# Loads of q, k and v split from one transfer for two head pairs into one per pair: a study of a linear-attention and token-mixing kernel

## Chip, cores, metric

One core of one Trainium2 chip. The metric is device time of one execution in microseconds (us). The kernel before takes 133.86 us (median of 3 runs, 133.42 to 133.96). "Span" is the profiled execution, a little shorter than the timed one.

## The reference

```python
# q, k, v: (8, 8, 576, 64) f32: batch, heads, sequence, head size
r = np.maximum(x, 0); phi(x) = concat([r * cos_w, r * sin_w])   # cos, sin of pi/2 * position / 576
kv  = einsum('bhsf,bhsd->bhfd', phi(k), v);  z = sum(phi(k), axis=2)
num = einsum('bhsf,bhfd->bhsd', phi(q), kv)
x   = num / (einsum('bhsf,bhf->bhs', phi(q), z)[..., None] + 1e-6)   # then heads side by side: (8, 576, 512)
wq, wk = x @ w_q, x @ w_k                                            # 512 -> 64
mixed  = einsum('bst,btd->bsd', einsum('bsd,btd->bst', wq, wk) / 8, x)
out    = np.maximum(mixed, 0) @ w_out                                # (8, 576, 512) f32
```

29.6 MB are read and 9.4 MB written.

## The kernel before

The work is cut into 16 units H; one unit is four heads, two "pairs" of two heads. A raw tile of one tensor and one unit has 128 partitions, 2 pairs, 576 columns of f32: 128 x 2 x 2304 B = 576 KB, with the two pairs side by side in a partition. It comes in one DMA. Six raw buffers are used in turn. All but a few DMAs are issued by SyncE, loads and stores in one queue.

```python
inp     = ctx.enter_context(tc.tile_pool(name="inp", bufs=PLAN["nraw"]))        # 6 raw buffers
outpool = ctx.enter_context(tc.tile_pool(name="outpool", bufs=PLAN["nout"]))    # 10 result buffers
...
def load(H, parts=((0, C9),), names=("q", "k", "v"), engs=()):
    ...
    b, h0 = divmod(2 * H, NPAIR)
    for nm in names:
        raw[nm, H] = inp.tile([P, 2, HC], FP32, name="raw")
    for lo, hi in parts:
        for nm in names:
            eng = nc.scalar if lo == 0 and nm in engs else nc.sync
            eng.dma_start(raw[nm, H][:, :, lo * D:hi * D],
                          srcs[nm][b][:, h0:h0 + 2, lo * D:hi * D])
...
def raw_c(nm, H, lo, hi):                 # what a cast reads: columns of BOTH pairs
    return raw[nm, H].rearrange("p i (c d) -> p c i d", c=C9)[:, lo:hi]
...
def store(bp, rt, qs):                    # a result tile of 128 x 512 f32: two DMAs of 64 partitions
    for hi in range(2):
        qs[hi].dma_start(
            dataclasses.replace(out, offset=out.offset + out_dest(bp, rt, hi),
                                ap=[[C9 * DM, 64], [1, DM]]),
            o_sbs[bp, rt][64 * hi:64 * hi + 64, :])
```

POOL (GpSimd) casts each raw tile, DVE multiplies k by the cosines, PE does the rest. The order of all instructions is fixed by a planner in the kernel.

Of the kernel before, what the change touches and what calls it, by code (L numbers as in the profile page):

```python
# [5 lines left out]

# [174 lines left out]
def kernel(  # L181
# [12 lines left out]
    B, NH, S, D = q.shape  # L194
# [37 lines left out]
    srcs = {}  # L232
# [3 lines left out]
    raw = {}  # L236
    CS = ((0, 5), (5, C9))

    def load(H, parts=((0, C9),), names=("q", "k", "v"), engs=()):
        if H >= NB:  # L240
            return
# [3 lines that stand above are left out]
        for lo, hi in parts:  # L245
            for nm in names:
                eng = nc.scalar if lo == 0 and nm in engs else nc.sync
                eng.dma_start(raw[nm, H][:, :, lo * D:hi * D],
                              srcs[nm][b][:, h0:h0 + 2, lo * D:hi * D])

    load(0, parts=CS, engs=("k",))

    warm = consts.tile([P, 512], BF16)
# [302 lines left out]
    def emit(n, eng, m):  # L556
        kind, b, j = n[0], n[1], n[2] if len(n) > 2 else 0
        if kind == "load":
            load(j, names=(b,))
        elif kind == "load_w":  # L560
            load_w(b)
# [91 lines left out]
```

## Time and profile before

| | before |
|---|---|
| time, median | 133.86 us |
| span of the profiled run | 130.8 us |
| mean PE clock granted | 0.974 of full |
| transfers in all; issued by SyncE from 40 to 90 us | 126; 61 |
| last load of k lands | 94.7 us |

The prediction below shows the views that it rests on; where it speaks of the first or second "pair" or of one "pair" of loads, it means a unit H. Beside those views, the page of the kernel before has these lines: PE's busy time, the PE clock in 40 slices (tenths of full speed), and the groups of issues (KB of one transfer, median us from issue to landing).

```profile
PE 105.8 (81%) x2279; PEld 61.8 (47%) x2279; DVE 93.8 (72%) x153; ACT 78.5 (60%) x154; POOL 76.8 (59%) x121
PEclk9999999999959999999999999999999999999995
raw<-in_k_dram SPq DMA_DIRECT2D x15, 576.0 KB, 7.3
out_dram<-o_sb SPq DMA_DIRECT2D x67, 128.0 KB, 5.3
```

The view by windows (window, its length, busy us of PE, PEld, DVE, ACT and POOL with counts, then the granted PE clock, the DMA share and GB/s):

```profile
48.00:56.00 8.00, 7.78 (x162) 4.56 (x156) 7.65 (x13) 5.07 (x12) 7.83 (x10) 1.00 1.05 400
64.00:72.00 8.00, 7.69 (x194) 4.89 (x193) 7.57 (x14) 4.83 (x11) 6.22 (x8) 1.00 1.03 394
40.00:90.00 50.00, 45.41 (x1123) 28.12 (x1122) 43.96 (x72) 35.12 (x73) 41.10 (x52) 1.00 1.03 375
```

### The profile page before, as it was taken

Reading aid. Unit: us, or ns where it says so; the run is one execution under the profiler, and the core shown is the slowest. Engines: PE = TensorE matmul, PEld = TensorE weight load, DVE = VectorE, ACT = ScalarE, POOL = GpSimd, SP = SyncE. Lnnn points to the kernel's source line nnn. Section 1 sums busy time; section 2 is a strip of 40 time slices with the busy share of each in tenths; the row PEclk is TensorE's granted clock in tenths of the full one; section 3 lists DMA queues with packets and bytes.
Section 4 is the critical chain, followed back from the end, with each engine's and each line's share of the span. In section 5 each row is a group of like instructions: output and inputs, shape, how many; then the busy total and the mean of one; then the engine's idle time right before and its main releaser. Section 6 shows DMA issues by size and latency. Waiting matters only on the chain.

```text
span 130.8 us, 5363 instructions
## 1 busy us (share of the span) xinstructions
PE 105.8 (81%) x2279; PEld 61.8 (47%) x2279; DVE 93.8 (72%) x153; ACT 78.5 (60%) x154; POOL 76.8 (59%) x121
## 2 busy tenths in 40 slices
PE   5947685885699989986999699889947999899930
PEld 2325253563546546643756366556624664443300
DVE  1065979689994999959999987989659876346200
ACT  6950063658756796639557595787637865655440
POOL 7728988896779999975697876885371000000000
PEclk9999999999959999999999999999999999999995
DMA  3999999999999999999999999999974034837973
GB/s 88 369 383 394 345 310 403 394 388 390 389 393 388 374 391 396 401 378 376 316 393 413 368 359 378 383 373 295 382 214 87 5 80 89 177 75 167 211 226 110
DMA packets 21239, 39.40 MB, mean 301 GB/s; under 512 B 3040, under 2 KB 4576, under 8 KB 21216
## 3 DMA queue, kind: packets, MB, share of 16 engines
q1 hardware_dynamic: 20544, 38.08, 85.0%
q10 hardware_dynamic: 672, 0.98, 2.5%
q8 instruction: 18, 0.29, 0.9%
q14 instruction: 5, 0.04, 0.1%
HBM read 29.62 MB, written 9.44 MB: 299 GB/s over the span
## 4 chain that ended last, share of the span: by engine, by line
PE 43%; DMA 23%; DVE 14%; ACT 5%; POOL 5%; issue 4%; SPq 2%; ACTq 1%; POOLq 0%
PE ps L532 19%; DMA raw<-in_k_dram 12%; DMA raw<-in_q_dram 9%; PE ps L422 5%; PE ps L462 5%; PE ps L397 5%; DVE kp L361 4%; DVE qpt_buf L389 4%; PE ps L492 3%; POOL rk L348 3%; PE ps L447 2%; PE ps L383 2%; DVE x_sb L435 2%; PE ps L508 2%; POOL rq_buf L348 2%
## 5 line engine op out<-in xcount | busy, mean ns | idle before, releaser
L532 PE MATMUL ps<-wo_sb,mix_sb 128*128 128x512 bf16 x144 | 37.3, 386 | 2.0 <-issue 1.7
L348 POOL TENSOR_SCALAR rq_buf<-raw 128x640 bf16<-128x640 f32 (+1 forms) x32 | 26.2, 835 | 9.3 <-DMA raw<-in_q_dram 7.9
L373 POOL TENSOR_SCALAR v_buf<-raw 128x640 bf16<-128x640 f32 (+1 forms) x30 | 27.1, 920 | 7.4 <-DMA raw<-in_v_dram 6.6
L361 DVE TENSOR_TENSOR kp<-rk,cossin 128x2304 bf16<-128x2304 bf16 (+2 forms) x17 | 22.5, 1324 | 11.3 <-ACT rk L346 6.1
L335 ACT COPY o_sb<-ps 128x512 f32<-128x512 f32 x32 | 18.8, 586 | 15.8 <-PE ps L532 12.9
L435 DVE TENSOR_TENSOR x_sb<-ps,rec 128x640 bf16<-128x640 f32 x32 | 26.4, 824 | 1.1
L389 DVE TENSOR_TENSOR qpt_buf<-ps,cst 128x1152 bf16<-128x1152 bf16 x32 | 22.6, 747 | 0.0
L348 POOL TENSOR_SCALAR rk<-raw 128x640 bf16<-128x640 f32 (+1 forms) x30 | 19.5, 669 | 4.2 <-DMA raw<-in_k_dram 2.7
L422 PEld LDWEIGHTS <-qpt_buf 64*128 64x128 bf16 x640 | 14.3, 95 | 14.0 <-issue 13.2
L422 PE MATMUL ps<-kv_sb,qpt_buf 64*128 64x65 bf16 x320 | 16.3, 193 | 4.2 <-DVE x_sb L435 3.7
L532 PEld LDWEIGHTS <-mix_sb 128*128 128x128 bf16 x144 | 11.9, 98 | 15.6 <-issue 4.1
L335 ACT COPY xT_buf<-ps 128x640 bf16<-128x640 bf16 (+1 forms) x25 | 15.7, 650 | 3.0 <-PE ps L447 1.7
L422 PE MATMUL ps<-kv_sh,qpt_buf 64*128 64x65 bf16 x320 | 16.3, 192 | 1.1 <-issue 0.2
L397 PE MATMUL ps<-v_buf,kp 64*128 64x65 bf16 x576 | 13.1, 190 | 3.8 <-DVE qpt_buf L389 2.9
L520 ACT ACTIVATE mix_sb<-ps 128x576 bf16<-128x576 f32 x24 | 14.7, 657 | 2.4 <-PE ps L508 2.4
L397 PEld LDWEIGHTS <-kp 64*128 64x128 bf16 x576 | 10.6, 94 | 8.2 <-issue 3.4
L335 ACT CAST kv_sb<-ps 128x260 bf16<-128x260 f32 x13 | 4.9, 378 | 12.4 <-PE ps L397 12.2
L508 PE MATMUL ps<-wT_buf,kx 64*128 64x288 bf16 x32 | 8.5, 292 | 2.6 <-ACT mix_sb L520 1.9
L258 PE MATMUL ps<-warm 128*128 128x512 bf16 x31 | 9.4, 441 | 1.5 <-DVE warm L254 1.5
L383 PE MATMUL ps<-ident,rq_buf 64*128 64x64 bf16 x288 | 8.1, 192 | 2.6 <-POOL rq_buf L348 1.3
L433 DVE RECIPROCAL rec<-ps 128x10 f32<-128x10 f32 x32 | 6.8, 213 | 4.0 <-PE ps L426 3.8
L462 PE MATMUL ps<-xT_buf,wqk_sb 128*128 128x288 bf16 x64 | 9.2, 287 | 0.0
(51 smaller groups left out, 115.8 us busy)
## 6 DMA issues: line engine op xcount, KB each, us to landing
raw<-in_q_dram SPq DMA_DIRECT2D x15, 576.0 KB, 7.1
raw<-in_k_dram SPq DMA_DIRECT2D x15, 576.0 KB, 7.3
raw<-in_v_dram SPq DMA_DIRECT2D x15, 576.0 KB, 7.2
out_dram<-o_sb SPq DMA_DIRECT2D x67, 128.0 KB, 5.3
wo_f<-in_moe_w_out_dram SPq DMA_DIRECT2D x1, 1024.0 KB, 10.2
out_dram<-o_sb ACTq DMA_DIRECT2D x5, 128.0 KB, 2.9
raw<-in_k_dram ACTq DMA_DIRECT2D x1, 320.0 KB, 4.5
raw<-in_q_dram SPq DMA_DIRECT2D x1, 320.0 KB, 4.2
```

Of the source, the lines that this page charges most:

```text
L335: nc.scalar.copy(dst, src)
L348: eng.tensor_scalar(dst, src, FMAX, 0.0, op0=ALU.min, op1=ALU.max)
L361: nc.vector.tensor_mul(kp[H][:, 2 * lo:2 * hi], rks[H][:, lo:hi].rearrange("p c i d -> p (c i) d").unsqueeze(2) .to_broadcast([P, 2 * (hi ...
L373: eng.tensor_scalar(dst, src, 1.0, 1.0, op0=ALU.mult, op1=ALU.mult)
L389: nc.vector.tensor_mul(qpt_bufs[H % 2][:, r, :, D:SLOTS * D], bank_h(K0 + r)[:, 0:1, 0:HC].to_broadcast([P, 2, HC]), cst)
L397: nc.tensor.matmul(bank(K0 + r)[:, 0, i * (D + 1):(i + 1) * (D + 1)], kp[H][half_rows(r), 2 * c + i, :, :], v_bufs[H % 3][half_rows(r), c, ...
L422: nc.tensor.matmul(nb[t][:, u, :], qpt_bufs[H % 2][rows, r, w, u * P:(u + 1) * P], mv, start=(u == 0 and w == 0), stop=False)
L435: nc.vector.tensor_tensor(xv[:, h, r], nv[:, :, :, 0:D], rec.to_broadcast([P, 2, SC, D]), op=ALU.mult)
L462: nc.tensor.matmul(bank(m + nh)[:, 0, 0:hs], wqk_sb[:, dmc, :, :], xT_bufs[b % 2][:, dmc, nh * hs:(nh + 1) * hs], start=(dmc == 0), stop=( ...
L508: nc.tensor.matmul(bank(m + r)[:, 0, 0:hs], kxs[b][half_rows(r), i * P:(i + 1) * P], rhs, start=True, stop=True)
L520: nc.scalar.activation(dst, src, AF.Relu, scale=scale_moe)
L532: nc.tensor.matmul(bank(m)[:, 0, :], mixs[bp][:, dmc, rt * P:(rt + 1) * P], wo_sb[:, dmc, :], start=(dmc == 0), stop=(dmc == NDM - 1))
```

## The change

Each 576 KB load becomes two of 288 KB, one per pair. The idea is a finer grain: shorter transfers that land sooner.

```diff
-                eng.dma_start(raw[nm, H][:, :, lo * D:hi * D],
-                              srcs[nm][b][:, h0:h0 + 2, lo * D:hi * D])
+                for i in range(2) if H else (slice(0, 2),):
+                    eng.dma_start(raw[nm, H][:, i, lo * D:hi * D],
+                                  srcs[nm][b][:, h0:h0 + 2, lo * D:hi * D][:, i])
```

The first unit keeps its loads. (The diff also adds an unused `import random`.)

More of the change, by code (lines that the diff above doesn't have):

```diff
@@ L4 @@
 import os
+import random
 from contextlib import ExitStack
```

## The prediction

> **What bounds the kernel now.** I read the page first. Its DMA row and its rate row cut the span in two.
>
> ```profile
> DMA  3999999999999999999999999999974034837973
> GB/s 88 369 383 394 345 310 403 394 388 390 389 393 388 374 391 396 401 378 376 316 393 413 368 359 378 383 373 295 382 214 87 5 80 89 177 75 167 211 226 110
> DMA packets 21239, 39.40 MB, mean 301 GB/s; under 512 B 3040, under 2 KB 4576, under 8 KB 21216
> ```
>
> A slice is 130.8/40 = 3.27 us. From about 3 to 95 us the 16 DMA engines are at least 90% busy and move some 380 GB/s; then the loads are over and a tail of PE work remains (PE is busy 7.92 of the 8 us from 104 to 112 in the view by windows). Next I asked whether anyone waits for these loads. POOL casts every raw tile from the second pair on; its timeline towards the end of the loads (start, duration, instruction; in brackets the idle time before it and what ended that):
>
> ```profile
> 88.66 1.80 POOL L373 TENSOR_SCALAR v_buf<-raw 128x640 bf16<-128x640 f32 x2 [0.76 <-DMA raw<-in_v_dram]
> 93.39 1.30 POOL L348 TENSOR_SCALAR rq_buf<-raw 128x640 bf16<-128x640 f32 x2 [2.94 <-DMA raw<-in_q_dram]
> 94.86 1.29 POOL L348 TENSOR_SCALAR rk<-raw 128x640 bf16<-128x640 f32 x2 [0.17 <-DMA raw<-in_k_dram]
> 96.93 1.78 POOL L373 TENSOR_SCALAR v_buf<-raw 128x640 bf16<-128x640 f32 x2 [0.78 <-DMA raw<-in_v_dram]
> ```
>
> POOL starts each cast when its load lands. The chain that ended last has the same piece in it (start, duration, what):
>
> ```profile
> 86.64 0.25 SPq L248
> ...
> 86.99 7.73 DMA raw<-in_k_dram
> ...
> 94.86 1.30 POOL rk L348 x2
> ...
> 96.19 1.36 DVE kp L361
> ```
>
> So the end is set by when the last loads land, about 93 to 97 us, plus a tail of some 34 us. PE is nearly as full: 50.83 of the 56 us from 40 to 96.
>
> The changed thing is how loads are issued, so the third view is SyncE's queue: its timeline for a stretch in which loads and stores alternate, a run of five stores near the end, and its waits from 40 to 90 us (total, times, longest).
>
> ```profile
> 67.28 0.54 SPq L248 DMA_DIRECT2D raw<-in_k_dram  x1
> 68.53 1.14 SPq L542 DMA_DIRECT2D out_dram<-o_sb  x2
> 69.76 0.56 SPq L248 DMA_DIRECT2D raw<-in_v_dram  x1
> ```
>
> ```profile
> 119.46 3.12 SPq L542 DMA_DIRECT2D out_dram<-o_sb  x5
> ```
>
> ```profile
> SPq L542 <- DMA raw<-in_q_dram: 3.8, 4, 1.0
> SPq L248 <- DMA raw<-in_v_dram: 2.5, 4, 1.1
> SPq L248 <- POOL rq_buf L348: 2.5, 4, 1.2
> ```
>
> An issue occupies SyncE for half a microsecond, and five back to back take 3.12/5 = 0.62 us each. All rows of those waits sum to 21.2 of the 50 us. Several are a store waiting for an earlier load to land. The listing of the built program says why: eight completion semaphores are used in turn, and each issue waits for the transfer eight issues before it. SyncE issues in order, so it never has more than eight transfers outstanding.
>
> **What the Trainium skill says.** "DMA: Bandwidth & Descriptors", section "Rules for kernel authors", advises to coalesce many small transfers into one large one; the change goes the other way, though 288 KB is far from its 64 KB. The section "Why a DMA increments its semaphore by 16 and not by 1" says that each participating engine ends its share with one increment. The trace agrees: 126 transfers x 16 = 2016 tiny packets, and with the 1024 rows of 256 B of the two small weights that is the 3040 under 512 B above. "Issuing engines are not separate DMA queues" in the same page calls issue time usually small beside the transfer. Here it is not: 0.62 us against 288/576 of the 1.5 us between landings of consecutive loads (390 GB/s), 0.75 us.
>
> **The change part by part.**
>
> Bytes and data packets stay: a row of 2304 B per partition and pair is one packet either way. Added are 45 completions of 16 packets, 720. A load carries 16 data packets per increment on an engine, a store 4, yet the rate in windows with stores (400 GB/s from 48 to 56) is not below that without (389 from 24 to 32), so I charge nothing, at most 0.3 us.
>
> No work starts earlier: the cast of columns 0 to 4 reads both pairs, and in the built program its first instruction waits on both semaphores. The second wait costs POOL perhaps 0.05 us on a load, and it has slack between loads. The first pair (H = 0) keeps its loads, and compute order is unchanged.
>
> Issue slots: from 40 to 90 us SyncE issues 24 loads and 37 stores, 61; after, 48 + 37 = 85. The rest of the 50 us beside waits, 28.8 us, is 0.47 us an issue (part of each issue hides in a wait), the back-to-back figure 0.62. The 85 need between 85 x 0.47 = 40 us and 85 x 0.62 = 53 us; halfway is 46 us. It just fits, by eating most of the idle time of SyncE. Before 40 us there are no stores: 6 issues, 3.7 us, against 4.5 us of transfer for one pair, which fits.
>
> Depth: the 61 transfers hold 24 x 576 + 37 x 128 = 18,560 KB, 304 KB each; eight are 2.4 MB, 6.4 us at 390 GB/s, which is what their latency of 6 to 7 us is: queueing. After, 218 KB each, eight are 1.75 MB (1.79 million bytes), 4.6 us. An unloaded store takes 2.3 us from issue to landing (98 to 120 us), so the engines should still have 4.6 - 2.3 = 2.3 us in reserve. Waits of SyncE shorter than that stay hidden; the longest in the table is 1.2 us.
>
> Sum: bytes 0, completions 0.3, waits of POOL 0.1, and for SyncE falling behind an amount between 0 and 3.5 us. For the upper end: 53 - 50 = 3 us of excess, some 3 us of unavoidable waits for data, less about 2.5 us because a load issued late into a shallower queue lands sooner. I take a third of it, 1.1 us. Landing delay passes one to one to the end, because POOL, DVE and PE follow it on the chain. 133.86 + 1.1 + 0.3 = 135.3, shaded to 135.0 as PE could absorb some.
>
> **The rivals.** (1) *Wholly hidden*: the engines stay fed, latency drops from 7 to about 5 us, and the time is 133.9. For it: the reserve of 2.3 us; and lane waits, the bulk of SyncE's idle time, are waits for the engines to catch up and cost nothing. (2) *SyncE becomes the bound*: 0.62 us per issue is the true sustained cost, 53 us do not fit into 50, and DMA share falls below 1 from 40 to 95 us; with occasional issues of over 1 us (1.61 is the longest load issue in the trace), 137 to 139 us. Against it: a load after a load took only 0.44 us at 87 us. (3) *The DMA engines gain*: each half is one contiguous 288 KB of HBM, which might move faster. Against it: 390 GB/s is reached now and packets keep their size; it would make 133 at best, since below 40 us POOL's buffers pace the issues anyway.
>
> **Range and chances.** Between rivals 1 and 2 the mass lies nearer 1. Runs scatter by 0.5 us. Range 133.3 to 138.0. The 2% line for slower is 136.5, which needs most of rival 2: 0.22. Faster by 2% would need 131.2, with no mechanism behind it: 0.03.
>
> **What the profile after would show.** Packets 21239 + 720 = 21959, of them 3760 under 512 B. Load rows x30 of 288 KB with a landing time of 4 to 5.5 us instead of 7. SyncE's total wait from 40 to 90 us down from 21 to under 12 us. The last load of k landing within 2 us of 94.7. If DMA tenths fall to 8 or 7 between 40 and 95 us while SyncE waits for little, rival 2 is right. If waits on landings stay near 10 us, rival 1 is. I am wrong if the first 40 us change by over 1 us, or if the time moves while the loads land as before.

## The result and the profile after

| | before | after |
|---|---|---|
| time, median of 4 runs in the same session | 133.91 us | 142.5 us |
| span of the profiled run | 130.8 us | 141.5 us |
| mean PE clock granted | 0.974 | 0.908 |
| last load of k lands | 94.7 us | 102.4 us |
| from there to the end | 36.1 us | 39.1 us |
| waits of SyncE from 40 to 90 us | 21.2 us | 10.7 us |

The ratio is 1.067 (95% interval 1.059 to 1.075): slower. Here and below a ratio is the mean time of one kernel's fast runs over the mean of the other's fast runs of the same rounds, so not quite the ratio of the medians quoted. The prediction had 135.0 and a range of 133.3 to 138.0: it was wrong. The two profiled executions took 132.56 and 143.6 us, the slowest of its four; they are 11.0 us apart where the medians are 8.6 apart, so the splits by profile below are somewhat too large.

The page after, rows that answer to those of before:

```profile
PEclk9999999997589999999999599959985569999996
DMA  3999999999999999999999999989866031755974
GB/s 105 370 390 390 347 373 390 368 390 393 393 390 381 300 324 285 311 315 251 313 337 356 354 351 339 378 275 281 281 200 155 5 74 34 153 116 129 199 215 129
DMA packets 21960, 39.41 MB, mean 279 GB/s; under 512 B 3760, under 2 KB 5296, under 8 KB 21936
raw<-in_k_dram SPq DMA_DIRECT2D x30, 288.0 KB, 5.6
```

A slice is now 141.5/40 = 3.54 us. Up to slice 13 (46 us) nothing changed: some 390 GB/s. From there to the end of the loads the rate is 250 to 380. The row above it hides this: the DMA share stays at nine tenths. The windows say it again:

```profile
48.00:56.00 8.00, 7.83 (x182) 4.84 (x181) 7.83 (x13) 5.39 (x13) 7.29 (x8) 1.00 0.95 302
64.00:72.00 8.00, 6.58 (x152) 4.13 (x151) 6.14 (x12) 3.38 (x7) 3.73 (x6) 1.00 0.94 296
104.00:112.00 8.00, 5.48 (x126) 4.10 (x126) 6.65 (x11) 3.63 (x8) 1.79 (x2) 0.57 0.41 102
40.00:90.00 50.00, 43.40 (x999) 26.15 (x998) 38.79 (x63) 30.50 (x64) 32.96 (x45) 0.96 0.98 329
```

A fall of the rate by a quarter (394 to 296) goes with a fall of the share by a tenth (1.03 to 0.94). The share counts the time that packets are under way, and slow packets count as busy: from 40 to 90 us, packets of 2304 B that took over 300 ns (their median is 93) fill 5.6 us of each of the 16 engines' time after the change and 2.4 us before. **Read GB/s, not share**, to see whether the engines are fed.

POOL's timeline at the end of the loads (start, duration, instruction; in brackets idle time and its end), and the piece of the chain that answers to the one in the prediction:

```profile
99.05 1.35 POOL L350 TENSOR_SCALAR rq_buf<-raw 128x640 bf16<-128x640 f32 x2 [1.82 <-DMA raw<-in_q_dram]
102.57 1.30 POOL L350 TENSOR_SCALAR rk<-raw 128x640 bf16<-128x640 f32 x2 [2.16 <-DMA raw<-in_k_dram]
104.63 1.79 POOL L375 TENSOR_SCALAR v_buf<-raw 128x640 bf16<-128x640 f32 x2 [0.77 <-DMA raw<-in_v_dram]
```

```profile
96.33 6.07 DMA raw<-in_k_dram
102.57 1.31 POOL rk L350 x2
103.90 1.36 DVE kp L363
```

The same three casts stand 5.7 to 7.7 us later. So 7.7 of the 10.7 us of span are lost before the last k lands, and 3.0 after. The chain's shares turned over: before "PE 43%; DMA 23%", after "DMA 57%; PE 15%".

The 3.0 us: PE waits more while loads are late, and its clock is halved in some stretches. Leaving out the last few us of a run, stretches at half clock sum to 3.4 us in the kernel before and to 24 us in the changed one; the one from 105.2 to 115.4 us lies at the start of the tail, after PE had waited from 103.2 us on. The Trainium skill, "TensorE: Matmul & The Clock Gate", Part 1, says that a monitor halves PE's clock after an idle window of about 3.4 us. The trace agrees in the length, for the half-clock stretches are 3.4, 6.8 or 10.2 us long; but such a window need not be empty: in the 3.4 us before each of the four stretches PE was busy for 1.4 to 1.7 us. At half clock for 10.2 us, PE loses 5.1 us of clock, an estimate that is enough for the longer tail, in which PE is not busy all the time. No experiment isolated it, so this share is read, not shown.

SyncE's waits from 40 to 90 us, largest first, and its timeline (start, duration, issues):

```profile
SPq L544 <- ACT mix_sb L522: 1.5, 2, 1.1
SPq L250 <- DMA raw<-in_q_dram: 1.2, 4, 0.3
```

```profile
44.49 0.83 SPq L250 DMA_DIRECT2D raw<-in_k_dram  x2
45.42 2.99 SPq L250 DMA_DIRECT2D raw<-in_v_dram  x2
48.51 1.05 SPq L250 DMA_DIRECT2D raw<-in_q_dram  x2
51.98 1.93 SPq L544 DMA_DIRECT2D out_dram<-o_sb  x2
```

SyncE now waits half as long as before, and many issues stand back to back. Some are long: the second half of v at 45.84 us took 2.58 us, while a 16 KB instruction fetch was under way from 45.88 to 48.04 (PE's by all appearance; the trace names its queue, 8, and not the engine); such an issue ends some 0.4 us after the fetch. The kernel before has them too (1.61 us at 58.9).

At this point two theories were open, and two more had to be excluded.

- **A**: SyncE's issue time. 85 issues, some of them blocked by fetches, do not fit into 50 us.
- **B**: depth. Each issue waits for the transfer eight issues earlier, so at most eight are outstanding (both traces have eight completion semaphores and never more than eight transfers outstanding). With the transfers that the kernel before issues from 40 to 90 us, the mean one shrank from 304 to 218 KB, and eight of them from 2.43 to 1.75 MB. (From here on "the limit" is this product, in units of 1000 KB.)
- C: the halved loads are slow in themselves.
- D: PE's clock alone.

### The profile page after: what moved, and what is told of

It reads as the page before. It is cut to its first block, busy times and chain, and to the rows that moved or that the text cites. A ratio compares the mean times of both kernels' runs of the same rounds, so it can differ in the third digit from the quotient of the medians.

```text
span 141.5 us, 5415 instructions
## 1 busy us (share of the span) xinstructions
PE 113.6 (80%) x2279; PEld 65.8 (47%) x2279; DVE 94.5 (67%) x153; ACT 78.7 (56%) x154; POOL 74.7 (53%) x121
## 2 busy tenths in 40 slices
DMA packets 21960, 39.41 MB, mean 279 GB/s; under 512 B 3760, under 2 KB 5296, under 8 KB 21936
## 4 chain that ended last, share of the span: by engine, by line
DMA 57%; PE 15%; SPq 6%; DVE 6%; POOL 5%; issue 3%; ACT 3%; ACTq 2%; POOLq 0%
DMA raw<-in_k_dram 20%; DMA raw<-in_q_dram 18%; DMA raw<-in_v_dram 8%; DMA out_dram<-o_sb 7%; PE ps L534 7%; SPq L250 5%; DMA wq_f<-in_moe_w_q_dram 4%; POOL rk L350 3%; ACT o_sb L337 2%; DVE qpt_buf L391 2%; PE ps L464 2%; DVE kp L363 2%; ACTq L544 2%; PE ps L424 1%; PE ps L399 1%
## 5 line engine op out<-in xcount | busy, mean ns | idle before, releaser
L534 PE MATMUL ps<-wo_sb,mix_sb 128*128 128x512 bf16 x144 | 40.5, 413 | 0.7 <-ACT o_sb L337 0.5
L375 POOL TENSOR_SCALAR v_buf<-raw 128x640 bf16<-128x640 f32 (+1 forms) x30 | 25.6, 869 | 11.1 <-DMA raw<-in_v_dram 7.8
L350 POOL TENSOR_SCALAR rq_buf<-raw 128x640 bf16<-128x640 f32 (+1 forms) x32 | 25.5, 813 | 10.7 <-DMA raw<-in_q_dram 9.3
L424 PEld LDWEIGHTS <-qpt_buf 64*128 64x128 bf16 x640 | 15.0, 98 | 21.3 <-issue 20.2
L399 PE MATMUL ps<-v_buf,kp 64*128 64x65 bf16 x576 | 15.1, 203 | 3.6 <-DVE qpt_buf L391 2.5
L399 PEld LDWEIGHTS <-kp 64*128 64x128 bf16 x576 | 12.2, 102 | 8.7 <-issue 3.7
L260 PE MATMUL ps<-warm 128*128 128x512 bf16 x31 | 10.2, 472 | 1.5 <-DVE warm L256 1.5
L510 PE MATMUL ps<-wT_buf,kx 64*128 64x288 bf16 x32 | 9.1, 319 | 2.2 <-ACT mix_sb L522 1.6
L510 PE MATMUL ps<-wq,kx 64*128 64x288 bf16 x32 | 9.3, 321 | 1.1 <-DVE wq L475 0.8
L464 PE MATMUL ps<-xT_buf,wqk_sb 128*128 128x288 bf16 x64 | 9.9, 301 | 0.0
```

What stands on the lines that cost most here:

```text
L350: eng.tensor_scalar(dst, src, FMAX, 0.0, op0=ALU.min, op1=ALU.max)
L375: eng.tensor_scalar(dst, src, 1.0, 1.0, op0=ALU.mult, op1=ALU.mult)
L399: nc.tensor.matmul(bank(K0 + r)[:, 0, i * (D + 1):(i + 1) * (D + 1)], kp[H][half_rows(r), 2 * c + i, :, :], v_bufs[H % 3][half_rows(r), c, ...
L424: nc.tensor.matmul(nb[t][:, u, :], qpt_bufs[H % 2][rows, r, w, u * P:(u + 1) * P], mv, start=(u == 0 and w == 0), stop=False)
L464: nc.tensor.matmul(bank(m + nh)[:, 0, 0:hs], wqk_sb[:, dmc, :, :], xT_bufs[b % 2][:, dmc, nh * hs:(nh + 1) * hs], start=(dmc == 0), stop=( ...
L510: nc.tensor.matmul(bank(m + r)[:, 0, 0:hs], kxs[b][half_rows(r), i * P:(i + 1) * P], rhs, start=True, stop=True)
```

## The experiments

Eighteen kernels ran. All of a group ran on the same chip, with the kernel before beside them. The scatter of that kernel follows PE's clock (130.25 us at clock 0.979, 139.15 at 0.903 on the first chip), so only fast runs are compared. They are few: one to four of each test kernel, and in group 3 two of the seven of the kernel before (131.11 and 132.6 us; the median of the seven is 134.64). A rate or a wait is read from one profile each, and those of e2, e4, e6, e7, e10 and e18 are of slow runs. In the first group a single run of before was fast, so no ratio is quoted for it; its kernels are compared with each other and with that 130.25.

### Group 1: issue time added, issues taken away

**e1**: time of SyncE alone, by semaphore increments that nobody waits for.

```diff
+                if H > 2:
+                    for _ in range(25):
+                        nc.sync.sem_inc(spare)
```

> The kernel before, its loads whole (576 KB), with 25 increments of a spare semaphore put on SyncE behind each load from the fourth pair on (17 ns each in the trace of before, with gaps an estimated 0.5 to 0.8 us in all). It adds issue-queue time, but no transfer, no packet, no completion semaphore, no half load. Theory A (SyncE's time per issue is what costs): with 24 x 0.5 to 0.8 = 12 to 19 us more to do in the 50 us from 40 to 90, SyncE is the bound as in the changed kernel; 139 to 147 us. Theory B (eight halves outstanding are too few bytes) and theory C (half loads or their extra completions move slower): unchanged, 133 to 135 us.

Measured: 160.84 us; the increments took about 1.5 us a load, 24 x 1.5 = 36 us in a stretch in which SyncE had 21 us to spare. SyncE's waits fell to 2.8 us and the rate to 272 GB/s. An overdose: it shows that SyncE can be made the bound, not that the change did it.

**e2**: the changed kernel, the second store of each tile issued by ACT.

```diff
-            store(b, j, (nc.sync, A if last else nc.sync))
+            store(b, j, (nc.sync, A))
```

> The changed kernel, with the second store of every pair of stores issued from ScalarE's queue. Transfers, their sizes, the semaphores in turn of eight and so the bytes outstanding are those of the changed kernel; SyncE has 18 issues fewer from 40 to 90 us. Theory A: 18 x 0.62 = 11 us less on SyncE, its load falls to 67 issues or 42 us, and most of the loss is won back: 134 to 137 us (ScalarE pays some 10 us of issue time in that stretch, of which it has 17 idle). Theory B: nothing changes in depth, 141 to 144 us. Theory C: 141 to 144 us.

Measured: 144.14 us, nothing recovered, though SyncE waited 25.2 us from 40 to 90 us, more than in the kernel before. The window from 40 to 90 us:

```profile
40.00:90.00 50.00, 38.60 (x840) 23.30 (x848) 34.93 (x56) 26.43 (x55) 35.30 (x45) 0.90 0.97 329
```

SyncE has time again, and the rate is 329 GB/s, that of the changed kernel (here in a slow run). This speaks against A. A weakness: ACT issues in order as well, and its stores can wait behind its own work.

**e3**: the changed kernel with one 256 KB store of 128 partitions per tile. The rows go to wrong places.

```diff
-        for hi in range(2):
-            qs[hi].dma_start(
-                dataclasses.replace(out, offset=out.offset + out_dest(bp, rt, hi),
-                                    ap=[[C9 * DM, 64], [1, DM]]),
-                o_sbs[bp, rt][64 * hi:64 * hi + 64, :])
+        qs[0].dma_start(
+            dataclasses.replace(out, offset=out.offset + (2 * bp * S + P * rt) * DM,
+                                ap=[[DM, P], [1, DM]]),
+            o_sbs[bp, rt])
```

> The changed kernel with each 128-row result tile stored by one DMA of 256 KB in place of two of 128 KB. The rows go to the wrong places of the output on purpose (each row written once, the result is wrong), bytes and packets are the same. Loads stay halved. Theory A: 48 + 18 = 66 issues from 40 to 90 us, 41 us: 133 to 136 us. Theory B: eight transfers hold 281 KB on average in place of 218, so B too expects most of the loss back, 134 to 137 us. Theory C: the loads are as slow as before, 140 us or more. It separates C from the two others.

Measured: 129.93 us (fast runs 128.27 to 130.0), 392 GB/s from 40 to 90 us. With halved loads the kernel is as fast as the kernel before: C is refuted. The window:

```profile
40.00:90.00 50.00, 43.64 (x1108) 28.01 (x1120) 45.21 (x72) 34.97 (x73) 41.95 (x53) 1.00 1.04 392
```

This store relieves both A (66 issues instead of 85) and B (279 KB on average, limit 2.23 MB).

**e4**: only q is halved (the diff is against the changed kernel): 69 issues, 269 KB, limit 2.15 MB.

```diff
-                for i in range(2) if H else (slice(0, 2),):
+                for i in range(2) if H and nm == "q" else (slice(0, 2),):
```

> Only the loads of q are halved. Theory A: 61 + 8 = 69 issues from 40 to 90 us, 69 x 0.62 = 43 us and some 5 us of long issues: it still fits, 133.5 to 136 us, far less than a third of the 8.6 us (a threshold). Theory C: a third of the loss, 136.5 to 137.5 us. Theory B: 8 transfers hold 269 KB on average, between the two, 134 to 137.

Measured: 135.26 us, fast runs 133.71 to 134.25, 345 GB/s. A part of the change costs a part of the loss, which A and B both allow.

### Group 2: A and B apart

**e5**: as e1, with 9 increments, so that SyncE loses as much time as the change takes.

> The kernel before, with nine semaphore increments on SyncE after each load from the fourth pair on: about 0.55 us more per load, 24 loads from 40 to 90 us, so 13 us of SyncE's time there, as much as the 24 added issues of the change take (24 x 0.5 = 12 us); the transfers, their sizes and the depth of eight are as before. Theory A (it is SyncE's time alone): ratio to before 1.05 to 1.07, waits of SyncE from 40 to 90 us near 10 us as in the changed kernel (10.7), rate below 330 GB/s. Theory B (it is the shallower queue of 8 x 218 KB, which no longer bridges issues blocked by an instruction fetch): depth is whole here, so the ratio is 0.99 to 1.015, rate near 380 GB/s. Both needed: 1.015 to 1.04.

**e6**: the kernel before with a limit of six instead of eight transfers, by an added dependence.

```diff
+    def behind(d, deep=6):
+        if len(issued) >= deep:
+            tc.add_manual_dep(d.ins, issued[-deep].ins.name, ...)
+        issued.append(d)
```

`behind` is called for each load from the fourth unit on and for each store but those of the last batch pair.

> The kernel before, where every load from the fourth pair on and every store but those of the last batch pair waits for the transfer six issues before it instead of eight: at most 6 x 304 KB = 1.82 MB outstanding, the depth of the changed kernel (8 x 218 KB = 1.75 MB); number and size of issues as before. Theory B (depth): ratio 1.04 to 1.07, rate from 48 to 72 us 300 to 330 GB/s, latency of loads 5.5 to 6 us. Theory A (SyncE's time): the added waits end when the engines have caught up, ratio 0.99 to 1.015. Both needed: 1.015 to 1.04.

The windows from 40 to 90 us, e5 first, e6 second:

```profile
40.00:90.00 50.00, 45.52 (x1062) 27.64 (x1061) 42.98 (x69) 32.97 (x68) 40.26 (x51) 0.96 1.01 363
```

```profile
40.00:90.00 50.00, 42.54 (x940) 25.50 (x938) 36.92 (x62) 29.03 (x60) 30.82 (x43) 0.90 0.92 300
```

Measured: e5 135.56 us, ratio 1.010 (1.000 to 1.021); e6 143.05 us, ratio 1.058 (1.047 to 1.068). In e5 SyncE waits only 9.6 us, less than in the changed kernel, and at most 2% is lost. In e6 it waits 24 us, issues as many and as large transfers as before, and the loss is there. **Theory A falls as the main cause; B stands.** (The profile of e6 fell into a slow run, so its 300 GB/s is a little low; the times are those of fast runs.)

The traces say the same without a new kernel. Counted every 0.05 us from 40 to 90 us, the transfers issued and not yet landed were 7.4 on average in the kernel before and 7.2 in the changed one, of eight; in e1, where SyncE is the bound, 3. SyncE keeps the places of the changed kernel nearly full; there are fewer bytes in them.

**e7**: e3 plus ten increments after each store but the last: SyncE as loaded as in the changed kernel, the limit 2.23 MB.

> The changed kernel with one 256 KB store per result tile in place of two of 128 KB (rows go to wrong places on purpose, so the result is wrong), plus ten semaphore increments (about 0.6 us) after each store but the last batch pair's: SyncE has the load of the changed kernel again, while the queue is deeper (48 x 288 + 18.5 x 256 KB over 66 issues = 281 KB, eight are 2.25 MB). Without the increments the same kernel took 129.93 us. Theory A: the pauses bring the loss back, ratio to before 1.03 to 1.07. Theory B: little of it comes back, ratio 0.97 to 1.01.

Measured: 133.09 us (129.5 to 134.46; one run fast). SyncE waits 7.9 us, the rate is 363 GB/s (e3: 392). A part of e3's gain may be gone, but none of the loss against the kernel before is there (134.51 us on the same chip): against A again.

**e8**: the changed kernel, right result; two result tiles share one buffer, and a store takes the 64 rows of both (256 KB). The edit is shortened here.

```diff
-            qs[hi].dma_start(
-                dataclasses.replace(out, offset=out.offset + out_dest(bp, rt, hi),
-                                    ap=[[C9 * DM, 64], [1, DM]]),
-                o_sbs[bp, rt][64 * hi:64 * hi + 64, :])
+            qs[hi].dma_start(                      # d0: place of the first tile's rows; n = 2 tiles
+                dataclasses.replace(out, offset=out.offset + d0,
+                                    ap=[[C9 * DM, 64], [out_dest(bp, rt, hi) - d0, n], [1, DM]]),
+                o_sbs[bp, rt // 2][64 * hi:64 * hi + 64, 0:n, :])
```

> The changed kernel with a correct result, where two result tiles share one buffer and one transfer of 256 KB carries the 64 rows of both: 18.5 store issues fewer from 40 to 90 us, so 48 + 19 = 67 issues of 277 KB. Theories A and B both expect the loss to go: ratio to before 0.97 to 1.01. If halved loads were slow in themselves or PE's clock were lost for another reason, it stays above 1.03.

Measured: 135.42 us, ratio 1.007 (0.998 to 1.016). The window:

```profile
40.00:90.00 50.00, 44.00 (x1064) 26.91 (x1062) 42.72 (x71) 33.77 (x70) 40.10 (x52) 1.00 1.02 366
```

With the loads as the change made them, larger stores bring the limit back to 2.2 MB and nearly all of the loss goes, although SyncE waits 10.6 us, no more than in the changed kernel (10.7).

### Group 3: the dose

e9 and e10 are e6 with seven and five; e11 is the changed kernel with seven; e12 is the kernel before with e8's stores (limit 3.5 MB).

> The kernel before with seven transfers outstanding instead of eight: 7 x 304 KB = 2.13 MB. Theory B (the bytes that may be outstanding set the loss): between the kernel before (2.43 MB, ratio 1) and six outstanding (1.82 MB, 1.058), ratio 1.00 to 1.03. If the loss at six came from the added waits as such and not from bytes, seven gives nearly as much: above 1.04.

> The kernel before with five outstanding: 5 x 304 KB = 1.52 MB, less than in the changed kernel (1.75 MB). Theory B: loss larger than at six, ratio 1.09 to 1.14.

> The changed kernel with seven outstanding: 7 x 218 KB = 1.53 MB, as many bytes as the kernel before with five. Theory B: the same time as that one within 2%, so 1.09 to 1.14 of the kernel before. Theory A (SyncE's time alone) leaves it at the changed kernel's 1.067 (1.05 to 1.08). If bytes and SyncE's time add up, it is over 2% slower than the kernel before with five.

> The kernel before with a correct result, two result tiles in one buffer and one 256 KB transfer for the 64 rows of both: 24 + 19 = 43 issues of 434 KB from 40 to 90 us, so eight would be 3.5 MB. Theory B with a curve that still rises beyond 2.4 MB: ratio 0.96 to 0.985, rate near 400 GB/s. If 2.4 MB is already enough: 0.985 to 1.01.

Measured: e9 135.57 us, ratio 1.026 (1.010 to 1.043), a difference that is near the scatter: the median of all seven runs of the kernel before is 0.7% below it; e10 149.69 us, 1.127 (1.092 to 1.161); e11 146.4 us, 1.105 (1.069 to 1.141). The changed kernel with seven and the kernel before with five, both at 1.52 MB, differ by 2% with intervals that overlap, although one issues twice as many loads.

e12 was 135.92 us, 1.030 (1.015 to 1.045), not faster. Its rate is 390 GB/s and its last k lands at 94.1 us, so the queue was well fed. A store that waits for a second tile holds up what stands behind it in SyncE's order (one wait for ACT of 3.7 us), but the last load landed no later, and the loss stands in the tail, for a cause that no run isolates. Like e9 it is near the scatter (134.64 us). More depth than 2.4 MB gained no time here.

### Group 4: a store that was meant to be better

e3 had a limit below that of the kernel before and was no slower, so it was asked whether half-height stores are part of the cause. e13 and e14 should give its store with the right rows, in the changed kernel and the one before; e15 and e16 are these with a limit of six and four.

```diff
+        d0, d1 = out_dest(bp, rt, 0), out_dest(bp, rt, 1)
+        qs[rt % 2].dma_start(
+            dataclasses.replace(out, offset=out.offset + d0,
+                                ap=[[d1 - d0, 2], [C9 * DM, 64], [1, DM]]),
+            o_sbs[bp, rt])
```

> The changed kernel with one 256 KB store per result tile, both 64-row halves in one transfer, rows in their right places: 48 + 18.5 issues of 279 KB, eight are 2.23 MB. Theory B and the run with wrong rows (129.9 us): ratio to before 0.97 to 1.01; the rows' places should not matter. If the place of the rows made that run fast, 1.01 to 1.04, as the depth curve says for 2.2 MB.

> The kernel before with one 256 KB store per result tile, right rows: 24 + 18.5 issues of 437 KB, eight are 3.5 MB. If full-height stores are better in themselves: ratio 0.96 to 0.985 and the same as the changed kernel with such stores within 1%. If depth beyond 2.4 MB is worth nothing and stores are alike: 0.985 to 1.01.

> The changed kernel with one store per tile and six transfers outstanding: 6 x 279 KB = 1.67 MB. Theory B (bytes outstanding alone): 1.06 to 1.11 of the kernel before, rate 290 to 330 GB/s. Half-height stores as the cause: 0.97 to 1.02.

> The kernel before with one store per tile and four transfers outstanding: 4 x 437 KB = 1.75 MB, the changed kernel's depth, while SyncE has only 43 issues from 40 to 90 us. Theory B: 1.05 to 1.09 of the kernel before. Theory A or half-height stores as the cause: 0.97 to 1.02.

Measured: 266.58, 266.95, 269.96 and 267.35 us, twice the time, all results right. The rate row of the page of e14:

```profile
GB/s 233 388 350 391 390 389 339 218 169 139 126 117 142 150 121 199 132 167 94 280 137 129 54 210 129 51 54 54 51 54 51 51 51 51 51 51 51 51 51 36
```

The stores ran at 51 GB/s, about 2/16 of 390. The Trainium skill has it: "DMA: Bandwidth & Descriptors", section "Rules for kernel authors", says that an outermost dimension of size c below 16 confines the transfer to at most c engines. Here c was 2, and the trace agrees. The question stayed unanswered. No form of this store with the 64 rows outermost was run.

### Group 5: the depth again, with full-height stores

e17: e3 with a limit of six; e18: the kernel before with e3's store and a limit of four (437 KB each on average). Wrong rows in both.

> The changed kernel with one 256 KB store of 128 partitions per tile (wrong rows on purpose) and six transfers outstanding: 6 x 279 KB = 1.67 MB. Theory B (bytes outstanding alone): 1.06 to 1.11 of the kernel before, rate 290 to 330 GB/s from 40 to 90 us. If half-height stores are needed for the loss: 0.96 to 1.02, rate above 370 GB/s.

> The kernel before with the same store and four transfers outstanding: 4 x 437 KB = 1.75 MB, the changed kernel's depth, with 43 issues of SyncE from 40 to 90 us against its 85. Theory B: 1.05 to 1.09 of the kernel before. Theory A, or half-height stores as the cause: 0.96 to 1.02.

Measured: e17 137.77 us, ratio 1.031 (1.022 to 1.039); e18 142.74 us, 1.065 (1.055 to 1.075). The window of e18 from 40 to 90 us:

```profile
40.00:90.00 50.00, 40.98 (x928) 25.30 (x936) 37.48 (x62) 29.09 (x61) 31.09 (x45) 0.93 0.95 316
```

e18 has whole loads, half as many issues as the changed kernel, 36 us of waits of SyncE in 50, full-height stores, and nothing in common with the change but the limit of 1.75 MB. It loses what the change loses. e17 lost half of what bytes alone would give against the kernel before; against its own parent e3 (other session, 129.4 us mean of fast runs) it is some 6% slower. So the limit is what counts, but stores of 128 partitions need somewhat less of it.

### All together

The limit is the nominal one, and the rate is that of one profile (slow runs: e6, e10, e18). Not in the table are the kernels without a ratio (e1 to e4 and e7; e3 had 8 x 279 KB and 392 GB/s), e12 (8 x 437 KB, 390 GB/s, 1.030) and e13 to e16.

| kernel | limit | MB | GB/s, 40 to 90 us | ratio |
|---|---|---|---|---|
| before | 8 x 304 KB | 2.43 | 375 | 1 |
| e9 | 7 x 304 | 2.13 | 356 | 1.026 |
| e6 | 6 x 304 | 1.82 | 300 | 1.058 |
| after | 8 x 218 | 1.75 | 329 | 1.067 |
| e11, after | 7 x 218 | 1.53 | 314 | 1.105 |
| e10 | 5 x 304 | 1.52 | 277 | 1.127 |
| e8, after with double stores | 8 x 279 | 2.23 | 366 | 1.007 |
| e18, one store, few issues | 4 x 437 | 1.75 | 316 | 1.065 |
| e17, after with one store | 6 x 279 | 1.67 | 342 | 1.031 |
| e5, SyncE delayed, depth kept | 8 x 304 | 2.43 | 363 | 1.010 |

## Why the prediction was wrong, point by point

- **What bounds the kernel**: right. The last loads and a tail set the end.
- **Bytes, packets, completions**: right. 21960 packets were counted for 21959 predicted, 3760 under 512 B as predicted, and e3 shows that halved loads can run at 392 GB/s.
- **No work starts earlier**: right in that nothing was gained by the end; the same three casts at the end came 5.7 to 7.7 us later.
- **Issue slots**: the step was sound enough. From 40 to 90 us SyncE made 71 issues in 50 - 10.7 = 39.3 us, 0.55 us each, between the 0.47 and 0.62 of the prediction; some took up to 2.6 us, longer than it allowed for. But that time was not the main cost: e5 took as much from SyncE and lost 1% (0 to 2%), e2 gave it back and gained nothing.
- **Depth: this is the step that failed.** The prediction put it that the engines "should still have 4.6 - 2.3 = 2.3 us in reserve" and that "Waits of SyncE shorter than that stay hidden". It saw the right quantity, 2.4 MB against 1.75 MB, and judged the smaller one enough, because an unloaded store lands in 2.3 us. That duration, of one small transfer with idle engines, is no measure of what a loaded queue needs: from 40 to 90 us stores of the changed kernel took 4.9 us (median) to land. Nor did short waits stay hidden: SyncE waited less than before, never over 1.1 us at a time, and the rate fell from 375 to 329 GB/s all the same. In the runs the loss begins near 2.2 MB, hardly below what the kernel before has: 1.007 at 2.23, 1.026 at 2.13, 1.058 at 1.82, 1.127 at 1.52.
- **One to one to the end**: mis-sized. 7.7 us at the last k became 10.7 at the end; the other 3.0 stand in the tail, at a halved PE clock.
- **The sum** charged 1.1 us for SyncE and nothing for depth; the loss was 8.6 us of median time (142.5 - 133.91).
- **Rival 1** said that waits for landings are "the bulk of SyncE's idle time"; in the rows of the kernel before they sum to 11.0 of 21.2 us.
- **Rival 2** (SyncE the bound, 137 to 139 us) was nearest in size and wrong in mechanism; at the end of its own list, "If DMA tenths fall to 8 or 7", it also watched the row that hardly shows it.
- **The first 40 us** did not change, as said; there are no stores there, and nearly all that is in the queue are loads (8 x 288 KB = 2.3 MB).
- Of the forecasts for the profile, SyncE's waits (under 12 us; 10.7) held; the landing time (4 to 5.5 us; 5.6 to 5.9) and the last k (within 2 us; 7.7 late) did not.

Why a limit of 1.75 MB starves engines whose transfers take under 6 us is not shown. The bytes issued and not yet landed follow the limit: 2.4 MB on average in the kernel before, 2.1 in e5, 1.9 in e6 and 1.6 in the changed kernel. The Trainium skill, "DMA: Bandwidth & Descriptors", section "Why a DMA increments its semaphore by 16 and not by 1", says that the up to 16 engines of a transfer finish independently, and a transfer has landed only when the last has. The trace agrees and has the size: for the transfers issued from 40 to 90 us, the last of the 16 increments came 2.1 us (median) after the first before the change and 2.05 us after it, while the time of a load from issue to landing fell from 7.1 to 5.1 us. So the part of its time in which a transfer holds one of the eight places while some engines are through with it grew. That these engines then run dry is not shown, for the trace does not name the engine of a packet. Nor are PE's instruction fetches the main cause: leaving out the stretches with a fetch and the 2.5 us after each, the changed kernel moves 333 GB/s from 40 to 94 us, and the kernel before 378.

No experiment found a right version that beats the kernel before. e3's store, with 392 GB/s, may point to one, but a correct form of it needs the rows of the result in another order, and that was not built.

## What to carry to other kernels

Where the number of outstanding transfers is fixed, cutting a transfer cuts the bytes in flight; work out number times mean size for the stretch that bounds, small stores included, and treat what the kernel has as needed until a run with one fewer shows otherwise. The cheap test is to lower the limit in the good kernel: here one transfer fewer cost 2.6% (1.0 to 4.3%), two fewer 5.8%. An issuing queue that waits much is no sign of a reserve (36 us of 50 in e18, which lost 6.5%), and the DMA share of a profile is no sign that the engines are fed; read GB/s.

## What the Trainium skill lacked or had wrong

- "DMA: Bandwidth & Descriptors" advises large transfers for the sake of each transfer's own cost; it has no word on how many bytes must be outstanding. Here 2.2 MB and more gave 363 to 392 GB/s on one core from 40 to 90 us, 1.75 MB 316 to 329 and 1.52 MB 277 to 314; between them the order is not clean (1.82 MB gave 300 in a slow run, 1.67 MB with stores of 128 partitions 342).
- The same page's "Issuing engines are not separate DMA queues" calls issue time usually small beside the transfer. An issue took 0.47 to 0.62 us against 0.75 us for a 288 KB transfer in a stream; yet the runs agree that it was not the main cost (e5, 1.010).
- No page has it that an issue of SyncE can stretch while instructions are fetched (on queue 8, probably PE's): 2.58 us at 45.84 us with a 16 KB fetch from 45.88 to 48.04 us. That the one causes the other is seen in time only.
- "Perfetto Trace Analysis", section "Identifying the Most-Contended Engine", already says to judge DMA by HBM utilization and not by occupancy. It lacks that slow packets keep the share up: 0.94 at 296 GB/s against 1.03 at 394.
- "TensorE: Matmul & The Clock Gate", Part 1, speaks of an idle window. Here PE was busy for 1.38 to 1.70 us of the 3.4 us before each halving of its clock, and the longest gap between its matmuls was 3.1 us (the changed kernel).
